# Attention heads with token-major scores and turned probabilities, every second head of two chunks

## The chip, the cores and the metric

The kernel runs on one core of a Trainium2 chip. The metric is the device time of one execution in microseconds (us), the median of three runs.

## The reference

A transformer block whose layer norms are modulated by a condition vector: attention of 2048 tokens over a cached window of keys and values, then a gated feed-forward part.

```python
mod = (_silu(c) @ w_mod).reshape(c.shape[0], 6, 1, -1)      # sa, ca, ga, sb, cb, gb
h = _layernorm(x, axis=-1) * (1 + ca) + sa
q = (h @ wq)                       # 2048 tokens, 32 heads of 128
k, v = k_cache[:, :, Sk - W:, :], v_cache[:, :, Sk - W:, :]  # 4 kv heads, W = 512 keys
scores = jnp.einsum('bhqd,bhkd->bhqk', q, k) * Dh ** (-0.5)
o = jnp.einsum('bhqk,bhkd->bhqd', _softmax(scores, axis=-1), v)
x = x + ga * (o @ wo)
h = _layernorm(x, axis=-1) * (1 + cb) + sb
x = x + gb * (silu(h @ w_gate) * (h @ w_up) @ w_down)
```

Everything is bfloat16; x is 2048x1024, wq 1024x4096, wo 4096x1024, the feed-forward width is 3584. Eight query heads share one kv head.

## The kernel before

The 2048 tokens are four chunks of 512. Attention comes first, chunk by chunk and head by head, in one loop `for i in range(1, NA + 2)` over NA = 128 pairs (chunk i // 32, head i % 32), which is software-pipelined. Iteration i projects q of pair i + 3 (`qproj`), computes the scores of pair i - 1 (`scores`) and the products with v of pair i - 2 (`pv`). After a chunk's last head, `oproj` multiplies by wo and adds to the residual. The feed-forward part follows for all chunks.

- `qproj`: eight matmuls of 128x512 into bank 4 (QB), then VectorE casts them to `qT_s` (L644). q lies feature-major: 128 features x 512 tokens.
- `scores`: four matmuls of 128x512 with a block of 128 keys as the stationary operand, so that the scores are key-major, in banks 0 to 3 (SCB); ScalarE takes the exponential in two instructions of 128x1024 (L813) into `ex_s`.
- `pv`: sixteen matmuls of 128x129. A 128x128 block of the exponentials is stationary, and v with a column of ones moves, so that the output is token-major and its last column is the sum of the exponentials. VectorE takes the reciprocal (L831) and multiplies (L834) out of banks 5 and 6; a DMA transpose (L837) brings the 512x128 result into `oT_all`, feature-major.
- `load_wq` fetches the weights for four heads (1 MB), `load_mt` and `mod_col` compute the late modulation columns beside attention (a DMA transpose from w_mod, then a VectorE reduction), and `run_bg` advances the layer norm of the next chunk by one step (`ln_task`, with a DMA transpose of 128x1024, L454).

The order of the work is the order in which the Python program records it; each engine, and the SP queue for its DMAs, runs its own instructions strictly in that order. A tracker sets the waits. Each buffer (`_Buf`) keeps the last write recorded and the reads since; in `T.op` a reader waits for that last write:

```python
for b in reads:
    lw = b.last_write
    if lw is not None:
        s, c = lw
        if req.get(s, 0) < c:
            req[s] = c
```

A write waits for the last write and for the reads recorded since it. `absorb` carries such waits over to another buffer that takes the same place in the arena.

Of the kernel before, what the change touches and what calls it, by code (L numbers as in the profile page):

```python
# [7 lines left out]
P = 128  # L8
# [122 lines left out]
def bass_adaLN_cond__sliding_block_cached__swiglu_ffn__prompt_kernel(  # L131
# [63 lines left out]
    rstd = [rstd4[:, i:i + 1] for i in range(4)]  # L195
    bq = S_("bq", [P, 8], F32)
    rl = [S_("rl%d" % i, [P, 4], F32) for i in range(2)]
    nsc = [S_("nsc%d" % i, [P, D], BF16) for i in range(2)]
    tmp = [S_("tmp%d" % i, [P, 512], F32) for i in range(2)]

    KB = 1024
    A_BYTES = 162 * KB
# [19 lines left out]
    def bank(b, n=512, off=0):  # L222
        return ps[:, b * 512 + off:b * 512 + off + n]
# [19 lines left out]
    B_mv = [_Buf("mv%d" % i) for i in range(4)]  # L243
    B_rs = [_Buf("rs%d" % i) for i in range(4)]
    B_rl = [_Buf("rl%d" % i) for i in range(2)]
    B_ns = [_Buf("ns%d" % i) for i in range(2)]
    B_tmp = [_Buf("tmp%d" % i) for i in range(2)]
    B_h2 = [[_Buf("h2_%d_%d" % (s, dt)) for dt in range(DT)] for s in range(2)]
# [12 lines left out]
    with nc.Block() as block:  # L261

        @block.gpsimd
        def _(g):
# [5 lines left out]
            def mm(out_ap, lhsT, rhs, start, stop, reads, bank_buf, skip=False):  # L270
                T.op(PE, lambda: TE.matmul(out_ap, lhsT, rhs, start=start, stop=stop, skip_group_check=skip),  # L271
                     reads=reads, writes=[bank_buf])
# [368 lines left out]
            def qproj(i, b=QB, k0=0):  # L641
                qproj_mm(i, b, k0, DT)
                qs = q_slot(i)
                T.op(DVE, lambda: V.tensor_copy(qT_s[qs], bank(b)), writes=[PB[b], B_qT[qs]])  # L644
# [160 lines left out]
            def scores(i):  # L805
                ch, h = divmod(i, Hq)
                gk = h // rep
                qs = q_slot(i)
                es = i % NEX
                for kt in range(KT):  # L810
                    mm(bank(SCB + kt), kT_sb[:, gk * KT + kt, :], qT_s[qs], True, True, [B_kT[gk], B_qT[qs]], PB[SCB + kt])
                for kp in range(KT // 2):
                    T.op(ACT, lambda: A.activation(ex_s[es][:, 2 * kp:2 * kp + 2, :], banks2(SCB + 2 * kp), AF.Exp, scale=att_scale),  # L813
                         writes=[PB[SCB + 2 * kp], PB[SCB + 2 * kp + 1], B_ex[es]])

            def pv(i):
                ch, h = divmod(i, Hq)
                gk = h // rep
                es = i % NEX
                os_ = i % NOS  # L820

                for jj in range(2):
                    for kt in range(KT):
                        for jb in range(2):
                            j = 2 * jb + jj
                            b = PVB + jb
                            mm(bank(b, P + 1, jj * 130), ex_s[es][:, kt, j * P:(j + 1) * P], v_aug[:, gk * KT + kt, 0:P + 1],
                               kt == 0, kt == KT - 1, [B_ex[es], B_va, B_vg[gk]], PB[b])
                both = [PB[PVB], PB[PVB + 1]]
                r = i % 2  # L830
                T.op(DVE, lambda: V.reciprocal(rl[r][:, :].rearrange("p (a b) -> p a b", a=2), psap(PVB * 512 + P, [[512, 2], [130, 2]])),  # L831
                     writes=both + [B_rl[r]])
                rlb = bass.AP(tensor=rl[r][:, :].tensor, offset=0, ap=[[4, P], [2, 2], [1, 2], [0, P]])
                T.op(DVE, lambda: V.tensor_tensor(o_s[os_].rearrange("p (a b) d -> p a b d", a=2),  # L834
                                                  psap(PVB * 512, [[512, 2], [130, 2], [1, P]]), rlb, ALU.mult),
                     reads=[B_rl[r]], writes=both + [B_os[os_]])
                T.op(Q_tr[os_], lambda: SP.dma_start_transpose(oT_all[:, h, :].rearrange("p (j q) -> p j q", j=TPC),  # L837
                                                               o_s[os_].rearrange("p j d -> p (j d)")),
                     reads=[B_os[os_]], writes=[B_oT[h]])

            B_wo = [_Buf("wo%d" % i) for i in range(8)]
            wo_s = [None] * 8
# [21 lines left out]
            def oproj_end(ch, k, b):  # L864
                j, hf = divmod(k, 2)
                t = ch * TPC + j
                resid(b, t, hf * 512, 512, 0, k, x_res[:, t, :], B_x[t])
                run_bg(1)

            def oproj(ch):  # L870
                for k in range(2 * TPC):
                    b = [QB, XB][k % 2]
                    oproj_mm(ch, k, b, 0, Hq)
                    oproj_end(ch, k, b)

            ln1 = {}
            ln2 = {}
# [15 lines left out]
            GATER = {19 + n: NGP + n for n in range(DT - NGP)}  # L893
            GATET = {23: 0, 24: 1}
            GATES = {26: 0, 27: 1}
            t2 = Hq + 6 + (9 * (NL - 1)) // 4
            TURNT = (28, t2 + 1)
            PUTT = {33: (0, c_sil, B_csil), 30: (1, mrow[0:DT, :], B_mrow), t2 + 3: (2, mrow[0:DT, :], B_mrow)}
            GETT = {35: (0, sc_row, B_scr), 31: (1, rowb[0][:, :], B_row[0]), t2 + 4: (2, rowb[1][:, :], B_row[1])}
            LOADT = {Hq + 2 + (9 * n) // 4: n for n in range(NL)}  # L900
            LOADO = {5 + (21 * p) // 8: p for p in range(8)}
            LOADK = {1: 1, 5: 2, 6: 3}
            for i in range(1, NA + 2):
                ch, h = divmod(i, Hq)
                if i in LOADK:
                    load_k(LOADK[i])
                if i == 4:
                    load_wq((i + 4) // 4 + 1)
                if 2 <= i < NQ0:
                    q_shifted(i)  # L910
                if i in (2, 3):
                    load_wga(i - 2)
                if i in LOADX:
                    load_x(LOADX[i])
                if i in LOADO:
                    load_wo(LOADO[i])
                if i in GATET:
                    gate_turn(GATET[i])
                if i in TURNT:
                    if i > Hq:  # L920
                        T.op(DVE, lambda: V.tensor_copy(mstg[:, 0:DT], mcol[:, 2 * DT:3 * DT]), reads=[B_mcol], writes=[B_mstg])
                    row_turn()
                if i in PUTT:
                    row_put(*PUTT[i])
                if i in GETT:
                    row_get(*GETT[i])
                if i == 7:
                    add_ln1(1)
                if h == 2 and 1 <= ch < NCH - 1:
                    add_ln1(ch + 1)  # L930
                if h == 2 and ch == NCH - 1:
                    add_ln2(0)
                if i + LEAD < NA:
                    if (i + LEAD) % Hq == 0:
                        finish(ln1[(i + LEAD) // Hq])
                    if i == 1:
                        scores(0)
                    if i in (1, 3, 5):
                        q_bias_mm(i + 1, i + 3, XB)
                    if i > NQ0:  # L940
                        qproj(i + LEAD)
                    elif i % 2 == 1:
                        qproj_mm(NQ0 + i // 2, QB, 0, HK)
                    else:
                        qproj(NQ0 - 1 + i // 2, QB, HK)
                if i - 4 in LOADT:
                    n = LOADT[i - 4]
                    mod_col(n)
                    g0, last = divmod(n, DT)
                    if last == DT - 1:  # L950
                        mod_take(g0, B_late[g0 + 1])
                        if g0 == 1:
                            mod_gain(1, B_late[2], B_g[1])
                n = i - (NA - LEAD)
                if 0 <= n <= 2:
                    oproj_mm(NCH - 1, 0, QB, 8 * n, 8 * n + 8)
                elif n >= 3:
                    oproj_mm(NCH - 1, 1, XB, 8 * (n - 3), 8 * (n - 3) + 8)
                if 1 <= i - 1 < NA:
                    scores(i - 1)  # L960
                if 0 <= i - 2 < NA:
                    pv(i - 2)
                    ch2, h2 = divmod(i - 2, Hq)
                    if i % 4 == 1 and i > 5:
                        load_wq((i + 4) // 4 + 1)
                    if i in LOADT:
                        load_mt(LOADT[i])
                    if h2 == Hq - 1 and ch2 < NCH - 1:
                        oproj(ch2)
                run_bg(1)  # L970
                for n in GATEP.get(i, ()):
                    gate_part(n)
                if i in GATER:
                    gate_row(GATER[i])
                if i in GATES:
                    gate_sum(GATES[i])
                if i == max(GATER):
                    gate_split()
# [152 lines left out]
```

## Time and profile before

| | |
|---|---|
| median of three runs | 1270.05 us (1269.99 to 1270.45) |
| profiled execution | 1270.14 us, of which span 1268.3 us |
| TensorE matmuls (PE) | 1255.1 us busy, 99% of the span |
| VectorE (DVE) | 485.1 us, 38% |
| ScalarE (ACT) | 341.6 us, 27% |
| 128x512 matmuls | 5085 records, mean 380 ns |
| 128x129 matmuls | 2048 records, mean 220 ns |
| DMA transposes of 128x512 (L837) | 128, median 2.6 us from issue to landing |

The span runs from the first to the last instruction of one profiled execution; the 1.8 us around it belong to the execution but to no instruction. Matmuls are pipelined: the duration of one in the table includes its way through the array, and the next one starts before it ends. PE is the matmuls, PEld the weight loads, SPq what the SP queue issues.

### The profile page before, as it was taken

How to read it: one execution, taken by the hardware profiler on the slowest of the kernel's cores; microseconds unless marked ns; L12 is line 12 of the kernel's file. 1: busy time of each engine (PE TensorE's matmuls, PEld its weight loads, DVE VectorE, ACT ScalarE, POOL GpSimd, SP SyncE). 2: the span in 40 equal slices, each digit the busy share in tenths (PEclk: the TensorE clock that was granted, in tenths of full speed). 3: DMA queues.
4: the chain of work that ended last, by engine and by line, in shares of the span. 5: the costliest groups of instructions: out<-in, count | busy, mean ns of one | idle time of the engine just before them, and what ended most of it. 6: DMA issues, size and time to landing. Idle time of an engine off the chain costs nothing.

```text
span 1268.3 us, 17609 instructions
## 1 busy us (share of the span) xinstructions
PE 1255.1 (99%) x7442; PEld 640.7 (51%) x7583; DVE 485.1 (38%) x894; ACT 341.6 (27%) x389; POOL 56.0 (4%) x95
## 2 busy tenths in 40 slices
PE   8999999999999999999999999999999999999999
PEld 5655545555455554555544444444444444444444
DVE  4676226764257641365322321233212321222122
ACT  4655205553035550155510111011100111011100
POOL 1530000000000000000000000000000000000000
PEclk9999999999999999999999999999999999999999
DMA  9998306875029641064243972055512644034200
GB/s 320 264 263 218 92 1 127 177 171 125 1 57 177 138 114 34 9 129 123 61 145 100 291 246 94 25 158 150 168 40 72 177 141 134 17 128 154 67 9 25
DMA packets 239997, 156.67 MB, mean 124 GB/s; under 512 B 133296, under 2 KB 225840, under 8 KB 239920
## 3 DMA queue, kind: packets, MB, share of 16 engines
q1 hardware_dynamic: 181664, 96.83, 31.6%
q10 hardware_dynamic: 58256, 58.73, 14.6%
q8 instruction: 59, 0.97, 0.3%
q14 instruction: 18, 0.15, 0.1%
HBM read 119.93 MB, written 4.20 MB: 98 GB/s over the span
## 4 chain that ended last, share of the span: by engine, by line
PE 98%; issue 1%; DMA 0%; SPq 0%; DVE 0%
PE ps L271 98%; DMA arena<-in_w_mod_dram 0%; SPq L309 0%; SPq L334 0%; PE ps L275 0%; DVE arena L496 0%; DVE tmp L853 0%; DVE arena L855 0%; DVE gain_f L486 0%
## 5 line engine op out<-in xcount | busy, mean ns | idle before, releaser
L271 PE MATMUL ps<-arena 128*128 128x512 bf16 (+1 forms) x7213 | 1249.3, 333 | 10.1 <-POOL arena L298 2.0
L271 PEld LDWEIGHTS ps<-arena 128*128 128x128 bf16 x7354 | 632.9, 98 | 621.5 <-issue 2.1
L813 ACT ACTIVATE arena<-ps 128x1024 bf16<-128x1024 f32 x256 | 261.9, 1023 | 345.1 <-PE ps L271 333.4
L1059 ACT ACTIVATE arena<-ps 128x512 bf16<-128x512 f32 x112 | 66.9, 597 | 499.6 <-PE ps L271 499.6
L1060 DVE TENSOR_TENSOR arena<-ps,arena 128x512 bf16<-128x512 f32 x112 | 77.5, 692 | 276.2 <-PE ps L271 276.2
L853 DVE TENSOR_TENSOR tmp<-ps,rowb 128x512 f32<-128x512 f32 (+1 forms) x65 | 44.4, 683 | 318.8 <-PE ps L271 318.8
L644 DVE CAST arena<-ps 128x512 bf16<-128x512 f32 x120 | 82.8, 690 | 47.7 <-PE ps L271 47.7
L834 DVE TENSOR_TENSOR arena<-ps,rl 128x512 bf16<-128x512 f32 x128 | 88.5, 691 | 4.7 <-DVE rl L831 0.2
L831 DVE RECIPROCAL rl<-ps 128x4 f32<-128x4 f32 x128 | 23.4, 182 | 114.1 <-PE ps L271 114.1
L429 POOL TENSOR_SCALAR rstd<-mv 128x1 f32<-128x1 f32 x28 | 6.1, 216 | 910.3 <-DVE mv L428 910.3
L424 DVE BATCH_NORM_STATS2 st<-x_res 128x6 f32<-128x512 bf16 x62 | 42.4, 683 | 3.4 <-DMA x_res<-in_A_x_dram 3.3
L593 DVE SCALAR_TENSOR_TENSOR arena<-arena 128x1024 bf16<-128x1024 bf16 x24 | 29.2, 1215 | 0.0
L855 DVE TENSOR_TENSOR arena<-tmp,x_res 128x512 bf16<-128x512 f32 (+2 forms) x33 | 22.3, 677 | 1.1
L855 DVE TENSOR_TENSOR x_res<-tmp,x_res 128x512 bf16<-128x512 f32 x32 | 22.2, 693 | 1.1
L440 DVE TENSOR_SCALAR arena<-arena,gain,mod_bf 128x512 bf16<-128x512 bf16 x56 | 21.2, 420 | 0.0
L435 DVE TENSOR_SCALAR nsc<-x_res,mv,rstd 128x1024 bf16<-128x1024 bf16 x30 | 19.2, 641 | 0.0
L431 POOL TENSOR_TENSOR rstd<-rstd,mhalf 128x1 f32<-128x1 f32 x28 | 15.7, 559 | 2.3
L772 POOL TENSOR_SCALAR arena<-arena,sc_bf 128x512 f32<-128x512 bf16 x8 | 12.9, 1614 | 0.5 <-POOL arena L774 0.2
L774 POOL TENSOR_TENSOR arena<-arena 128x512 f32<-128x512 f32 x8 | 10.1, 1265 | 0.7
L428 DVE BATCH_NORM_AGGREGATE mv<-st 128x2 f32<-128x12 f32 x28 | 5.8, 209 | 1.0
L271 PEld LDWEIGHTS ps<-sc_bf,arena 128*128 128x128 bf16 x128 | 4.4, 96 | 1.4 <-DMA arena<-in_w_mod_dram 0.3
L271 PE MATMUL ps<-sc_bf,arena 128*128 128x1 bf16 x128 | 4.7, 164 | 0.3 <-DMA arena<-in_w_mod_dram 0.3
(56 smaller groups left out, 59.4 us busy)
## 6 DMA issues: line engine op xcount, KB each, us to landing
arena<-in_A_wq_dram SPq DMA_DIRECT2D x30, 1024.0 KB, 5.8
arena<-in_B_w_gate_dram ACTq DMA_DIRECT2D x28, 1024.0 KB, 5.4
arena<-in_B_w_up_dram ACTq DMA_DIRECT2D x28, 1024.0 KB, 7.9
arena<-in_A_wo_dram SPq DMA_DIRECT2D x8, 1024.0 KB, 7.6
arena<-in_B_w_down_dram SPq DMA_DIRECT2D x7, 1024.0 KB, 8.3
out_dram<-arena SPq DMA_DIRECT2D x15, 256.0 KB, 2.0
x_res<-in_A_x_dram SPq DMA_DIRECT2D x3, 1024.0 KB, 7.0
arena<-arena SPq DMA_TRANSPOSE x132, 2.6
```

The lines of the kernel that those rows point to most:

```text
L271: T.op(PE, lambda: TE.matmul(out_ap, lhsT, rhs, start=start, stop=stop, skip_group_check=skip), reads=reads, writes=[bank_buf])
L424: T.op(DVE, lambda: V.bn_stats(st_[sl][:, hf * 6:hf * 6 + 6], x_res[:, t, hf * 512:hf * 512 + 512]), reads=[B_x[t]], writes=[B_st[sl]])
L440: T.op(DVE, lambda: V.tensor_scalar(dst[:, dt, :], dst[:, dt, :], gain[gi][:, dt:dt + 1], mod_bf[:, ccol + dt:ccol + dt + 1], op0=ALU.mult ...
L593: T.op(DVE, lambda: V.scalar_tensor_tensor(mt[n % 2], mt[n % 2], 1.0, sc_row, op0=ALU.mult, op1=ALU.mult, accum_out=mcol[:, n:n + 1]), rea ...
L644: T.op(DVE, lambda: V.tensor_copy(qT_s[qs], bank(b)), writes=[PB[b], B_qT[qs]])
L813: T.op(ACT, lambda: A.activation(ex_s[es][:, 2 * kp:2 * kp + 2, :], banks2(SCB + 2 * kp), AF.Exp, scale=att_scale), writes=[PB[SCB + 2 * k ...
L831: T.op(DVE, lambda: V.reciprocal(rl[r][:, :].rearrange("p (a b) -> p a b", a=2), psap(PVB * 512 + P, [[512, 2], [130, 2]])), writes=both + ...
L834: T.op(DVE, lambda: V.tensor_tensor(o_s[os_].rearrange("p (a b) d -> p a b d", a=2), psap(PVB * 512, [[512, 2], [130, 2], [1, P]]), rlb, A ...
L853: T.op(DVE, lambda: V.tensor_tensor(tmp[s][:, 0:n], bank(b, n), rowb[ri][:, c0:c0 + n], ALU.mult), reads=[B_row[ri]], writes=[PB[b], B_tmp ...
L855: T.op(DVE, lambda: V.tensor_tensor(dst[:, c0:c0 + n], tmp[s][:, 0:n], x_res[:, t, c0:c0 + n], ALU.add), reads=[B_tmp[s], B_x[t]], writes= ...
L1059: T.op(ACT, lambda: A.activation(sg_s[ss], bank(gb), AF.Silu), writes=[PB[gb], B_sg[ss]])
L1060: T.op(DVE, lambda: V.tensor_tensor(guT[:, ft, :], bank(ub), sg_s[ss], ALU.mult), reads=[B_sg[ss]], writes=[PB[ub], B_gu[ft]])
```

## The change

For every second head of the last two chunks (pairs 66, 68, ..., 126, the set `NAT`) the scores are computed token-major: a 128-token block of q is stationary, and the 512 keys move. ScalarE takes the exponential in four instructions of 128x512 and sums each row on the way (`accum_out`). VectorE takes the reciprocals of the sums and multiplies the probabilities with them, in two halves (`nat_norm`), and one DMA transpose of 128x2048 turns all of them (`nat_turn`). The products (`nat_pv`) then are four matmuls of 128x512 with a 128x128 block of v as the stationary operand; their output is feature-major, so ScalarE copies it straight into `oT_all`, and the transpose of the output goes away for these heads. Iteration i turns pair i and records the products of pair i - 4.

Two places hold probabilities before the turn (`pn`: the arena's `ex_s[0]` and the residual's `tmp`), two slots hold turned ones (`pt`); `p_slot` alternates between them. `pt_region` moves the two slots to another part of the arena at pairs 66, 86 and 96. At a chunk's seam (i = 65, 97) the scores of the next such pair lie inside `oproj`. `load_mt` starts one iteration earlier and then comes every second iteration, and from i = 65 on `load_wq` is recorded ahead of the scores.

```diff
+            NAT0 = 2 * Hq + 2
+            NAT = set(range(NAT0, NA, 2))
+            B_pn = [[_Buf("pn0_%d" % hf) for hf in range(2)], B_tmp]
+            pn = [None, tmp_t[:, :].bitcast(BF16)]
+            Q_pt = [dq("q_pt%d" % i) for i in range(2)]
+            def p_slot(i):
+                return (i - NAT0) // 2 % 2
+            def pt_region(off):
+                pt_over[:] = B_oT[24:] if off == OFF_OT + 24 * KB else []
+                for s in range(2):
+                    B_pt[s] = _Buf("pt%d" % s)
+                    pt[s] = arena.at(off + s * 4 * KB, [TPC * KT, P], BF16, [B_pt[s]])
+            def nat_scores(i):
...
+                for j in range(TPC):
+                    mm(bank(SCB + j), qT_s[qs][:, j * P:(j + 1) * P],
+                       kT_sb[:, gk * KT:(gk + 1) * KT, :].rearrange("p a b -> p (a b)"), True, True,
+                       [B_kT[gk], B_qT[qs]], PB[SCB + j])
+                for j in range(TPC):
+                    T.op(ACT, lambda: A.activation(pn[s][:, j * 512:(j + 1) * 512], bank(SCB + j), AF.Exp, scale=att_scale,
+                                                   accum_out=psum[s][:, j:j + 1]),
+                         writes=[PB[SCB + j], B_pn[s][j // 2], B_psum[s][j // 2]])
+            def nat_norm(i, hf):
+                s = p_slot(i)
+                T.op(DVE, lambda: V.reciprocal(pinv[s][:, 2 * hf:2 * hf + 2], psum[s][:, 2 * hf:2 * hf + 2]),
+                     reads=[B_psum[s][hf]], writes=[B_pinv[s][hf]])
+                for j in (2 * hf, 2 * hf + 1):
+                    pj = pn[s][:, j * 512:(j + 1) * 512]
+                    T.op(DVE, lambda: V.tensor_scalar(pj, pj, pinv[s][:, j:j + 1], None, op0=ALU.mult),
+                         reads=[B_pinv[s][hf]], writes=[B_pn[s][hf]])
+            def nat_turn(i):
+                s = p_slot(i)
+                pt_of[i] = (pt[s], B_pt[s], list(pt_over))
+                T.op(Q_pt[s], lambda: SP.dma_start_transpose(pt[s], pn[s]), reads=B_pn[s], writes=[B_pt[s]])
+            def nat_pv(i):
...
+                pa, pb, over = pt_of.pop(i)
+                ptv = pa.rearrange("p (j k) q -> p j k q", j=TPC)
+                for kt in range(KT):
+                    mm(bank(PVB).rearrange("p (j q) -> p j q", j=TPC), v_aug[:, gk * KT + kt, 0:P], ptv[:, :, kt, :],
+                       kt == 0, kt == KT - 1, [B_va, B_vg[gk], pb], PB[PVB])
+                T.op(ACT, lambda: A.activation(oT_all[:, h, :], bank(PVB), AF.Copy), writes=[PB[PVB], B_oT[h]])
...
-            LOADT = {Hq + 2 + (9 * n) // 4: n for n in range(NL)}
+            LOADT = {Hq + 1 + 2 * n: n for n in range(NL)}
+            PTAT = {2 * Hq + 2: OFF_OT + 24 * KB, 2 * Hq + 22: OFF_H20, 3 * Hq: OFF_HT}
...
+                if i % 4 == 1 and i >= NAT0 - 1:
+                    load_wq((i + 4) // 4 + 1)
...
+                seam = (i - 1) % Hq == 0 and i + 1 in NAT
+                if i + 1 in PTAT and not seam:
+                    pt_region(PTAT[i + 1])
+                if i in NAT and (i - 2) % Hq:
+                    nat_norm(i, 1)
+                    nat_turn(i)
+                nat = i % 2 == 1 and i + 1 in NAT
+                if nat and not seam:
+                    if i - 4 not in LOADT:
+                        run_bg(1)
+                    nat_scores(i + 1)
-                if 1 <= i - 1 < NA:
+                if 1 <= i - 1 < NA and i - 1 not in NAT:
                     scores(i - 1)
                 if 0 <= i - 2 < NA:
-                    pv(i - 2)
+                    if i - 4 in pt_of:
+                        nat_pv(i - 4)
+                    if i - 2 not in NAT:
+                        pv(i - 2)
+                    if (i - 2) % Hq == Hq - 1 or i == NA:
+                        for n in sorted(pt_of):
+                            if n < i:
+                                nat_pv(n)
+                    if nat and not seam:
+                        nat_norm(i + 1, 0)
...
-                        oproj(ch2)
+                        oproj(ch2, [lambda: nat_scores(i + 1), lambda: (nat_norm(i + 1, 0), nat_norm(i + 1, 1))] if seam else ())
+                        if seam:
+                            if i + 1 in PTAT:
+                                pt_region(PTAT[i + 1])
+                            nat_turn(i + 1)
```

## The prediction

> **What bounds the kernel now.** I read the page's engine table and its chain of waits first, then TensorE's waits, the groups by shape, the timeline of one attention iteration, and the landing times of the transposes.
>
> ```profile
> PE 1255.1 (99%) x7442; PEld 640.7 (51%) x7583; DVE 485.1 (38%) x894; ACT 341.6 (27%) x389; POOL 56.0 (4%) x95
> ...
> PE 98%; issue 1%; DMA 0%; SPq 0%; DVE 0%
> ```
>
> ```profile
> PE ps L271 <- POOL arena L298: 2.0, 1, 2.0
> PE ps L271 <- DVE arena L496: 0.6, 1, 0.6
> PE ps L271 <- DMA arena<-in_w_mod_dram: 0.3, 1, 0.3
> ```
>
> TensorE is the bound everywhere: 99% busy, 98% of the chain, and 2.9 us of waits in the whole span, all at the start. A change gains only by taking away TensorE time. It loses whatever it makes TensorE wait, because nothing else is on the path.
>
> ```profile
> 601.07 0.18 DVE L831 RECIPROCAL rl<-ps 128x4 f32<-128x4 f32 x1 [1.08 <-PE ps L271]
> 601.28 0.69 DVE L834 TENSOR_TENSOR arena<-ps,rl 128x512 bf16<-128x512 f32 x1
> 602.00 1.19 SPq L837 DMA_TRANSPOSE arena<-arena  x1
> 602.80 0.69 DVE L644 CAST arena<-ps 128x512 bf16<-128x512 f32 x1 [0.82 <-PE ps L271]
> 603.23 2.14 ACT L813 ACTIVATE arena<-ps 128x1024 bf16<-128x1024 f32 x2 [1.36 <-PE ps L271]
> 604.57 0.18 DVE L831 RECIPROCAL rl<-ps 128x4 f32<-128x4 f32 x1 [1.08 <-PE ps L271]
> ```
>
> This is one iteration of attention in the timeline: start, duration, engine, instruction. From RECIPROCAL to RECIPROCAL it lasts 3.50 us. The chain has 49 matmuls of 128x512 in 10.74 us (from 138.11); the last takes its own 0.38, so one step is (10.74 - 0.38)/48 = 0.216 us. Twelve of them (eight for the next q, four scores) are 2.59 us. The remaining 0.91 us are sixteen 128x129 products at 57 ns. RECIPROCAL starts about 0.20 us after the last product's step, so the iteration begins at E = 600.87. The CAST of q then runs from E+1.93 to E+2.62.
>
> **What is saved.** 31 heads (66, 68, ... 126) replace sixteen products (0.91 us) by four of 128x512 (0.86 us). That is 0.044 us a head, 31 x 0.044 = 1.4 us in all. The scores keep four matmuls of 512 columns. The gain is bounded there: a tenth of a per cent, less than the 0.2% (2.5 us) that a measurement of this kernel tells from no change.
>
> **What is added to TensorE's path: a wait.** This is the step that sets the forecast. There are two slots of turned probabilities, and `p_slot` gives heads i-4 and i the same one. In an even iteration the loop records `nat_turn(i)` first and `nat_pv(i-4)` after it. The tracker makes a reader wait for the last write recorded for its buffer, and that is now the turn of head i, not of head i-4. So the products meant to run four iterations behind wait for a transpose issued in their own iteration. I counted iterations by the slots: 70 to 84 (8), 90 to 94 (3) and 102 to 126 (13), 24 in all. At 86, 88 and 96 the slots have just moved to another place (`pt_region`), so the older turn is the last one written there; 66, 68, 98 and 100 have no product to make.
>
> What the turn waits for, in an even iteration beginning at E (the odd one began at E-3.50):
> - In the odd iteration VectorE ends the regular head's RECIPROCAL and TENSOR_TENSOR 4.61 us after its start, at E+1.11 (3.70 + 0.18 + 0.03 + 0.69). Then come `nat_norm(i,0)`'s reciprocal (0.18) and two 128x512 multiplies. The nearest row is this one, and I take its 0.41 us:
>
> ```profile
> L435 DVE TENSOR_SCALAR arena<-x_res,mv,rstd 128x512 bf16<-128x512 bf16 x2 | 0.8, 410 | 0.8 <-POOL rstd L528 0.8
> L541 ACT ACTIVATION_READ_ACCUMULATOR arena<-x_res,nmean 128x1 f32 x1 | 0.2, 186 | 0.0
> L1059 ACT ACTIVATE arena<-ps 128x512 bf16<-128x512 f32 x112 | 66.9, 597 | 499.6 <-PE ps L271 499.6
> ```
>
> - With 0.03 us between dependent instructions (1.06 us in all) that ends at E+2.20, so the q CAST, queued behind it, is done at E+2.92. Then `nat_norm(i,1)`, another 1.06 us: E+4.0. In the eight iterations of chunk 2 before i = 86 a `mod_col` (1.22 + 0.08) stands in the queue too and adds 0.25.
> - ScalarE is not late: its four exps of 0.60 + 0.19 us (the rows above) end 5.3 us after the odd iteration's start, E+1.8.
> - SP issues at E+4.03. SP is free by then: the regular head's transpose takes 1.19 and `load_mt` 1.3 from E+1.1 on, together to E+3.6.
> - The landing of a 128x2048 transpose is in no row. Nearest:
>
> ```profile
> L837 SPq DMA_TRANSPOSE arena<-arena x128: 1188/1192/2657, 35.0 to 639.6; - x128
> ...
> DMA to landing us min/median/max: 2.4/2.6/8.1
> ```
>
> ```profile
> L454 SPq DMA_TRANSPOSE arena<-nsc x28: 1232/1250/2732, 57.0 to 1018.1; - x28
> ...
> DMA to landing us min/median/max: 3.1/5.1/7.5
> ```
>
> These are 128x512 and 128x1024. Undisturbed, 2.4 and 3.1 us: twice the data costs 0.65 more, so four times gives about 4.35 at least. Two 128x1024 transposes issued back to back at 206.01 and 207.36 are down by 210.7, 4.7 us for the same data. Four of 128x512 in a row, 3 x 1.19 + 2.4 = 6.0, is the upper end. I take 4.5, between the first two, since it is one issue.
>
> Landing is at E+8.53; TensorE is ready at E+2.59. With 0.03 to wake and the mean of the 0.25 (0.08), the wait is 6.05 us. 24 x 6.05 = 145 us. Queued behind the waiting product on TensorE is everything: the next q, the next scores, the regular products. Nothing covers it.
>
> **Smaller additions.** At i = 97 three heads are finished in a row through one bank: `nat_pv(94)` waits for the regular head's eviction (0.20 + 0.18 + 0.03 + 0.69 = 1.1), the next for ScalarE's copy of the last (0.38 + 0.04 + 0.60 less the step, 0.8) and for turn 96, due about then: 1.9 us. At i = 128 the copy again, 0.8. Together 2.7. VectorE's and ScalarE's extra work (31 times a net 1.2 and 1.7 us), and the 31 dropped o transposes, lie inside iterations that the wait makes longer. `load_mt` every second iteration and the moved `load_wq` stay off the path: VectorE needs some 3.0 us of each 3.50 in chunk 1.
>
> **TensorE's pace after a wait.** Between 3.2 and 5.6 us, after the idle start, matmuls are slow; 0.38 us is their normal duration:
>
> ```profile
> L271 PE MATMUL ps<-arena 128*128 128x512 bf16 x6 | 2.7, 630 | 0.0
> ```
>
> Twelve of them fill 4.34 us from 3.10, where 11 x 0.216 + 0.38 = 2.75 would do; counted from the first at 2.02 the loss is about 2.1 us. A later gap of 0.55 us (at 10.65) is followed by normal durations. A 6 us gap lies between these rows: 0 to 2.1 us a stall. I take half, 1.05, as neither row is nearer: 25 us in 24 stalls.
>
> By the Trainium skill (TensorE: Matmul & The Clock Gate, "What's actually happening") the array halves its clock after an idle window of about 3.4 us and frees it after a busy one. By that a 6 us gap holds a whole window about three times in four, and the sum would be an estimated 13 us higher. No row in the span shows such a fall, only the slow start.
>
> **The sum.** The profiled execution took 1270.1 us (span 1268.3 and 1.8 around it), the median 1270.05. 1270.1 - 1.4 + 145 + 2.7 + 25 = 1442 us.
>
> **Rivals.**
> - *No loss of pace.* The gaps are too short to slow the array: 1270.1 - 1.4 + 145 + 2.7 = 1416 us. For it: nothing in the span shows a fall. Against: the start does run slow.
> - *Full loss of pace.* Each stall pays what the start paid, 24 x 2.1 = 50: 1467 us. The skill's rule above stands nearest to this one.
> - *A slow transpose.* Landing in 6.0 us or more; the maxima of 8.1 and 7.5 show what a neighbour's traffic can do. The stall is 7.55, 24 x 7.55 = 181: 1477 us with half the pace loss, 1502 with all. Against: the added `load_wq` traffic (5.8 us to landing) starts with the odd iteration and is down before the turn starts.
> - *No wait: not slower.* The products wait for the turn of four iterations before, as the change's words have it. Then 14 us cover a chain that ends 8.5 us after E, and 1270.1 - 1.4 + 2.7 = 1271.4 us remains, within 0.2%. It decides from the turn of head i: if TensorE doesn't need it until E+17, all 145 us and the pace loss vanish. Against it is the order of recording alone, but that I read as certain.
>
> **How the numbers follow.** Forecast 0.52, no pace loss 0.15, full pace loss 0.17, slow transpose 0.12, no wait 0.04. Low end: landing 4.35 and multiplies of 0.35 (row L675: 348 ns) make the stall 5.65, 136 us, with no pace loss: 1407. High end: the slow transpose with all the pace loss, 1502. I give 1405 to 1502. Slower by over 0.2% holds all but the no-wait case: 0.96; same 0.03; faster 0.01, since 1.4 us alone doesn't reach 0.2%.
>
> **What would show it.** Right: TensorE's waits list some 24 for a DMA (arena<-arena or arena<-tmp), about 6 us each, in chunks 2 and 3; heads 82, 84 and 92 have none; TensorE's busy share near 88%; granted clock below 1.00 from 530 us on. Each L896 issue lands in 4.4 to 4.7 us. Wrong: no such waits, or a share of these waits naming VectorE or ScalarE.

## The result, and the profile after

The changed kernel takes 1450.13 us (median of five runs, 1448.90 to 1451.89) beside 1270.05 us: a ratio of 1.1415 [1.1399, 1.1431]. The forecast of 1442 was 8 us short. The profiled execution took 1451.89 us, with a span of 1450.1 us and a mean granted clock of 0.962.

The page's engine table, chain of waits and clock row of the changed kernel (the clock in tenths, one digit for each fortieth of the span):

```profile
PE 1308.9 (90%) x7211; PEld 633.0 (44%) x7211; DVE 506.3 (35%) x1018; ACT 378.5 (26%) x606; POOL 56.0 (4%) x95
...
PEclk9999999999888889998988999999999999999999
...
PE 83%; DMA 9%; DVE 7%; issue 0%; ACT 0%; SPq 0%; ACTq 0%
```

TensorE is busy for 53.8 us longer and yet only 90% of the time; DMA now holds 9% of the chain and VectorE 7%. The clock row falls below 9 in eight slices between the 11th (from 362.5 us) and the 22nd (to 797.6 us), which is where the token-major heads are. TensorE's waits say on what (total us, times, longest):

```profile
PE ps L276 <- DMA arena<-arena: 70.6, 13, 7.9
PE ps L276 <- DMA arena<-tmp: 58.1, 11, 5.8
PE ps L276 <- ACT arena L907: 2.9, 3, 1.4
PE ps L276 <- POOL arena L303: 2.0, 1, 2.0
PE ps L280 <- DVE nsc L440: 1.6, 2, 1.3
PE ps L276 <- DVE arena L841: 1.0, 1, 1.0
PE ps L276 <- DMA arena<-in_A_wq_dram: 1.0, 2, 0.7
PE ps L276 <- DVE pinv L886: 0.9, 1, 0.9
```

13 + 11 = 24 waits for a transpose out of the two places `pn`, together 128.7 us, 5.36 each. The view of the turn's own line (L896) has both sides of it, the landing and who waited:

```profile
L896 SPq DMA_TRANSPOSE arena<-arena x16: 1532/1960/4108, 363.5 to 802.6; - x16
L896 SPq DMA_TRANSPOSE arena<-tmp x15: 1719/1932/2909, 375.0 to 789.6; - x15
...
PE ps L276: 128.7, 24
...
DMA to landing us min/median/max: 4.3/4.3/6.2
```

One stall in the timeline, in chunk 3 (start, duration, engine, instruction, idle time before it and what ended that):

```profile
677.20 0.69 DVE L841 TENSOR_TENSOR arena<-ps,rl 128x512 bf16<-128x512 f32 x1
...
677.99 0.74 DVE L890 TENSOR_SCALAR tmp<-tmp,pinv 128x512 bf16<-128x512 bf16 x2
...
678.71 0.69 DVE L649 CAST arena<-ps 128x512 bf16<-128x512 f32 x1
...
679.50 0.74 DVE L890 TENSOR_SCALAR tmp<-tmp,pinv 128x512 bf16<-128x512 bf16 x2
...
680.27 1.72 SPq L896 DMA_TRANSPOSE arena<-tmp  x1
...
684.62 3.40 PE L276 MATMUL ps<-arena 128*128 128x512 bf16 x8 [5.09 <-DMA arena<-tmp]
```

It is the chain of the forecast in its order: the regular head's eviction, the first half of the norm, the cast of q, the second half, SP's issue 0.03 us later, and 4.35 us on TensorE begins. The eight matmuls behind the wait take 3.40 us: a step of some 0.43 us, where 0.216 is the normal one. So the kernel loses twice at each of these places, by the wait and by the pace after it. The experiments separate the two.

### The profile page after: what moved, and what is told of

Its sections match the earlier page's. It is cut to its first block, busy times and chain, and to the rows that moved or that the text cites. A ratio compares the mean times of both kernels' runs of the same rounds, so it can differ in the third digit from the quotient of the medians.

```text
span 1450.1 us, 17431 instructions
## 1 busy us (share of the span) xinstructions
PE 1308.9 (90%) x7211; PEld 633.0 (44%) x7211; DVE 506.3 (35%) x1018; ACT 378.5 (26%) x606; POOL 56.0 (4%) x95
## 4 chain that ended last, share of the span: by engine, by line
PE 83%; DMA 9%; DVE 7%; issue 0%; ACT 0%; SPq 0%; ACTq 0%
PE ps L276 83%; DMA arena<-arena 4%; DMA arena<-tmp 3%; DVE arena L649 1%; DVE arena L841 1%; DVE arena L890 1%; DMA arena<-in_A_wq_dram 1%; DVE tmp L890 1%; DVE arena L598 0%; DVE st L429 0%; DVE rl L838 0%; DVE pinv L886 0%; DMA x_res<-in_A_x_dram 0%; SPq L593 0%; ACT arena L820 0%
## 5 line engine op out<-in xcount | busy, mean ns | idle before, releaser
L276 PE MATMUL ps<-arena 128*128 128x512 bf16 (+2 forms) x6982 | 1303.7, 350 | 137.1 <-DMA arena<-arena 70.6
L276 PEld LDWEIGHTS ps<-arena 128*128 128x128 bf16 x6982 | 625.4, 99 | 809.7 <-DMA arena<-arena 77.0
L820 ACT ACTIVATE arena<-ps 128x1024 bf16<-128x1024 f32 x194 | 198.7, 1024 | 275.7 <-PE ps L276 266.6
L1159 ACT ACTIVATE arena<-ps 128x512 bf16<-128x512 f32 x112 | 66.9, 597 | 500.2 <-PE ps L276 500.2
L841 DVE TENSOR_TENSOR arena<-ps,rl 128x512 bf16<-128x512 f32 x97 | 67.1, 692 | 3.4
L907 ACT ACTIVATE arena<-ps 128x512 bf16<-128x512 f32 x31 | 18.5, 596 | 138.0 <-PE ps L276 138.0
L838 DVE RECIPROCAL rl<-ps 128x4 f32<-128x4 f32 x97 | 17.7, 183 | 92.2 <-PE ps L276 92.2
L880 ACT ACTIVATE arena<-ps 128x512 bf16<-128x512 f32 x64 | 37.9, 595 | 44.1 <-PE ps L276 41.2
L880 ACT ACTIVATE tmp<-ps 128x512 bf16<-128x512 f32 x60 | 35.6, 595 | 31.6 <-PE ps L276 28.8
L890 DVE TENSOR_SCALAR arena<-arena,pinv 128x512 bf16<-128x512 bf16 x64 | 22.6, 353 | 2.3
L890 DVE TENSOR_SCALAR tmp<-tmp,pinv 128x512 bf16<-128x512 bf16 x60 | 21.2, 353 | 2.1
```

The lines of the kernel that those rows point to most:

```text
L880: T.op(ACT, lambda: A.activation(pn[s][:, j * 512:(j + 1) * 512], bank(SCB + j), AF.Exp, scale=att_scale, accum_out=psum[s][:, j:j + 1]), ...
L890: T.op(DVE, lambda: V.tensor_scalar(pj, pj, pinv[s][:, j:j + 1], None, op0=ALU.mult), reads=[B_pinv[s][hf]], writes=[B_pn[s][hf]])
L1159: T.op(ACT, lambda: A.activation(sg_s[ss], bank(gb), AF.Silu), writes=[PB[gb], B_sg[ss]])
```

## The experiments

**e1_order: the turn recorded behind the products.** Nothing is left out; the last norm half and the turn move behind `nat_pv(i-4)`, so that the products' last recorded write is the turn of their own head.

```diff
-                if i in NAT and (i - 2) % Hq:
-                    nat_norm(i, 1)
-                    nat_turn(i)
...
                     if i - 4 in pt_of:
                         nat_pv(i - 4)
+                    if i in NAT and (i - 2) % Hq:
+                        nat_norm(i, 1)
+                        nat_turn(i)
```

> The changed kernel with nat_norm(i,1) and nat_turn(i) recorded behind nat_pv(i-4), so that the products wait for the turn of four iterations before; nothing else. Theory (the loss is the wait for the turn of the same iteration, and the slow pace after it): the 24 waits for a DMA vanish, the granted clock is 1.00, and the time is 1270.1 - 1.4 + 2.7 = 1271.4 us, within 1270 to 1274. Rival (the new form itself costs: more VectorE, ScalarE and SP work, and four times the transposed data): most of the 180 us stays, over 1350 us.

Measured: 1279.17 us (four executions, 1276.22 to 1280.46), 1.0065 [1.0051, 1.0078] of the kernel before. TensorE's waits in the profiled execution, the slowest of the four:

```profile
PE ps L276 <- ACT arena L907: 3.0, 3, 1.5
PE ps L276 <- POOL arena L303: 2.0, 1, 2.0
PE ps L276 <- DMA arena<-in_A_wq_dram: 2.0, 1, 2.0
PE ps L276 <- DVE arena L841: 1.1, 1, 1.1
PE ps L276 <- DVE pinv L886: 0.9, 1, 0.9
PE ps L276 <- DVE arena L501: 0.6, 1, 0.6
PE ps L276 <- DMA arena<-in_w_mod_dram: 0.2, 1, 0.2
```

All 24 waits for a turn are gone, and 171 us with them: the order of recording is the cause. What is left is 8.7 us more than before and 7.8 more than I had expected. In the profiled execution, which is 10.0 us above the kernel before, 3.0 + 1.1 us are seams, where finished heads go through one bank; 2.0 us are a wait for the weights of q, 0.9 for the first norm; some 3 us are pace. The windows of the seam at i = 97 (length, busy time of PE, PEld, DVE, ACT and POOL with instructions, granted clock, DMA share, GB/s):

```profile
474.00:478.20 4.20, 2.33 (x23) 1.35 (x22) 1.57 (x3) 0.60 (x1) 0.00 (x0) 1.00 1.02 204
478.30:485.00 6.70, 6.01 (x15) 1.95 (x14) 0.00 (x0) 0.60 (x1) 0.00 (x0) 0.50 0.36 103
```

Behind gaps of 1.09 and 0.78 us the clock is at a half for 6.8 us; a third gap, of 0.69 us, lies inside that stretch. The other three executions have a granted clock of 1.000, which has no room for such a stretch (it makes 0.997 here), and yet they take 1276.22, 1278.80 and 1279.54 us. So pace is no part of the median's 8.7 us: the waits less the 1.4 us saved make 5.6 of it, and some 3 us stay open.

**e2_fill22, e3_fill8: the gap filled with work that nobody reads.** The wait stays as it is, but N matmuls of 128x512 into a free bank stand ahead of each waiting product: TensorE is kept busy while the turn is under way. Results are as in the changed kernel.

```diff
                     if i - 4 in pt_of:
+                        if i < NA and pt_of[i - 4][1] is B_pt[p_slot(i)]:
+                            for _ in range(22):      # 8 in e3_fill8
+                                mm(bank(PVB + 1), kT_sb[:, 0, :], kT_sb[:, 0:KT, :]..., True, True, [B_kT[0]], PB[PVB + 1])
                         nat_pv(i - 4)
```

> The changed kernel with 22 matmuls of 128x512, whose result nobody reads, ahead of the products in each of the 24 iterations that wait (22 x 0.216 = 4.75 us of a wait of about 5.1). Theory (of the 181 us, 129 are waits and some 54 are matmuls at half pace after them): the array stays busy, the clock stays at 1.00, the landing of the turn sets the time as before, and 54 us go: 1396 us. Rival (the clock has no part; what is lost is wait alone, and the busy time is an artefact of records): 1450 us, or more.

Measured: 1411.54 us, 1.1116 [1.1099, 1.1133], granted clock 0.999. Its waits for turns:

```profile
PE ps L276 <- DMA arena<-arena: 9.9, 12, 3.2
PE ps L276 <- DMA arena<-tmp: 5.9, 11, 0.8
```

22 useless matmuls in each of 24 places make the kernel 38.6 us faster. That is what the lost pace costs, 1.6 us a stall. The clock records agree: in the changed kernel's profile there are 24 slow stretches, one at each wait, TensorE is busy for 86.9 us in them, and at half clock half of that is lost, 43 us; e2_fill22 has one left, which costs 1.7 us. My 54 us was the growth of the page's busy time, and that was a wrong measure: the trace of the kernel before has 7442 matmuls for 7583 weight loads, so records are missing and its busy time is too short. Beside e4_seam (below), which has the same matmuls as the changed kernel, all 7211 recorded, at full clock, the busy time grows by 46 us (1262.9 to 1308.9). The wait alone is then e2_fill22 less e1_order, 132 us, or 5.5 us a stall; TensorE's waits in the profile, which begin at the end of the last matmul and not at its step, make 128.7.

> The same with 8 matmuls, 1.73 us of the wait; an idle gap of 3.3 to 3.8 us remains. Theory A (the clock falls only after a whole idle window of 3.4 us, as the changes of clock 3.41, 6.83 and 10.24 us apart suggest): most gaps no longer hold a window, the clock is above 0.99, and the time is 1396 to 1405 us, about as with 22. Theory B (the loss goes with the length of the gap): a third of the loss goes, 1450 - 54 x 1.73/5.3 = 1432 us.

Measured: 1448.36 us, 1.1405 [1.1388, 1.1421], clock 0.967. Eight matmuls take 1.7 us out of each gap and win nothing that can be told. The same window, two iterations long, in the changed kernel and then in e3_fill8:

```profile
686.00:699.65 13.65, 8.60 (x46) 3.91 (x45) 4.24 (x11) 5.29 (x11) 0.00 (x0) 0.88 0.49 110
```

```profile
686.00:699.65 13.65, 10.34 (x54) 4.70 (x52) 3.79 (x11) 5.30 (x13) 0.00 (x0) 0.87 0.36 67
```

There are eight more matmuls in the 13.65 us, and the clock is down as much. In the clock records of both kernels every slow stretch lasts 3.41, 6.83 or 10.24 us, whole multiples of one window of 3.413 us; both have 24 of them, and a pair of iterations in chunk 3 settles at 13.65 us, four such windows, with one slow stretch in each pair.

**e5_fill14, e6_fill18: between the two.** The same edit with 14 and 18.

> The changed kernel with 14 unread matmuls ahead of each waiting product (3.02 us), so that 2.1 to 2.6 us of the wait stay idle, after 22 matmuls took away all slow pace (1411.5 us) and 8 none of it (1448.4). Theory A (a window of 3.4 us that is idle for about two thirds slows the clock too, as the cold stretch behind three short gaps at the seam of e1_order suggests): many of the gaps still slow the array, granted clock about 0.97 to 0.98, 1425 to 1448 us. Theory B (only a wholly idle window does): no gap can hold one, granted clock above 0.99, 1411 to 1415 us.

> The same with 18 matmuls (3.88 us), 1.2 to 1.7 us of the wait idle, 35 to 50% of a window. Theory A (about two thirds idle is what it takes): hardly any fall, 1411 to 1418 us. Rival (a third is enough): still over 1425 us.

Measured: 1440.24 us, 1.1323 [1.1306, 1.1340] with 14, and 1411.93 us, 1.1114 [1.1099, 1.1128] with 18. The span and mean granted clock of 8, 14 and 18 fillers:

```profile
core 0: 1444.9 us, clock 0.967
```

```profile
core 0: 1438.6 us, clock 0.975
```

```profile
core 0: 1410.3 us, clock 0.996
```

With 14, gaps of 2.0 to 2.6 us are left at most places, and the clock falls at 19 of the 24; with 18, gaps of 1.1 to 1.8 us are left at most, and none of these costs anything (there are three slow stretches, two behind gaps of 3.95 and 2.83 us and one behind the gaps of the seam).

What decides is the idle time inside one window. In each trace all the slow stretches begin on one grid of 3.413 us. Laid over TensorE's gaps between 320 and 830 us, in the seven traces that have slow stretches there (the changed kernel, e1_order, the four fills and e10_half_fill16 below), every window outside a slow stretch that holds 2.02 us or more of idle time is followed by half pace, and none that holds less than 1.78 us is. In between both occur: 1.78 us at the seam of e6_fill18 was followed, 1.93 us in e1_order was not. A gap of 2.32 us in e5_fill14 cost nothing, since it lay in two windows with 1.66 and 0.66 us. So the step lies between 1.8 and 2.0 us of idle time in one window, a little over half of it.

It is a step: four more matmuls a stall are worth 28 us, the eight of e3_fill8 were worth nothing that can be told. With 0, 8, 14, 18 and 22 useless matmuls there are 24, 24, 19, 3 and 1 slow stretches, and half of TensorE's busy time in them is 43, 40, 34, 5 and 2 us; less that, all five kernels take 1406 to 1410 us.

**e10_half_fill16: half the data.** 16 fillers, and the turn moves only the first half of the probabilities (128x1024); the other half of the slot isn't written, so its time is that of a smaller transfer.

```diff
-                T.op(Q_pt[s], lambda: SP.dma_start_transpose(pt[s], pn[s]), ...)
+                T.op(Q_pt[s], lambda: SP.dma_start_transpose(pt[s][:, 0:TPC * KT // 2, :], pn[s][:, 0:TPC * KT // 2 * P]), ...)
```

> The changed kernel with 16 unread matmuls ahead of each waiting product, as in the runs with 18 and 22, and each turn moves only the first half of the probabilities (128x1024): the second half of what the products read is left out. Theory (the landing of the turn stands whole in each of the 24 waits, and nothing else ends them): landing 3.1 instead of 4.3 us, 24 x 1.2 = 29 us less than the full turn with a steady clock: 1411.7 - 29 = 1383 us. Rival (the wait ends by VectorE's or SP's backlog, not by the landing): 1405 us or more.

Measured: 1379.04 us, 1.0851 [1.0834, 1.0867], clock 0.999. The turn in it:

```profile
L896 SPq DMA_TRANSPOSE arena<-arena x16: 1231/1233/1953, 362.6 to 733.4; - x16
...
DMA to landing us min/median/max: 3.0/3.1/4.1
```

It takes 32.9 us less than e6_fill18. Some 3 us of that are pace (one slow stretch here, three there: 1.7 and 4.7 us by the clock records), so the wait is 30 us shorter, 1.25 a stall, for a landing that is 1.2 us shorter. The landing stands whole in the wait, as the sum had it.

**e4_seam: the seams mended as well.** e1_order, and the head that is finished at a chunk's seam gets the other bank in the next iteration.

```diff
-            def nat_pv(i):
+            def nat_pv(i, b=PVB):
...
-                    if (i - 2) % Hq == Hq - 1 or i == NA:
-                        for n in sorted(pt_of):
-                            if n < i:
-                                nat_pv(n)
+                    if i % Hq == 0 and i - 2 in pt_of:
+                        nat_pv(i - 2, PVB + 1)
```

> e1_order, and at the end of a chunk the two last products no longer stand in a row in one bank: nat_pv(94) and nat_pv(126) are recorded one iteration earlier in bank 6, and nat_pv(96), which belongs to the next chunk, stays with its turn at i = 100. Theory (the seams cost 2.7 us of e1_order, the four wide products save 1.4 us): 1268.7 us, 0.1% below the kernel before and 2 to 3 us below e1_order. Rival (there is no gain in four matmuls of 512 columns over sixteen of 129): 1270 us or above.

Measured: 1272.12 us, 1.0013 [1.0005, 1.0022], clock 1.000. The seams were worth 7.1 us, where I had put 2.7 in the forecast and 2 to 3 here: 4.1 us are the four gaps of e1_order's profile (1.09, 0.78, 0.69 and 1.51), and the rest stays open, as three of e1_order's four executions lost no pace. The waits for q's weights stay (1.4 us in two), and the timeline shows why: SP is behind in chunk 2.

```profile
409.11 0.57 SPq L362 DMA_DIRECT2D arena<-in_A_wq_dram  x1
...
411.08 2.54 SPq L593 DMA_TRANSPOSE arena<-in_w_mod_dram  x1
...
413.74 3.14 SPq L896 DMA_TRANSPOSE arena<-arena  x1
...
419.64 2.89 SPq L896 DMA_TRANSPOSE arena<-tmp  x1
...
423.93 0.57 SPq L362 DMA_DIRECT2D arena<-in_A_wq_dram  x1
```

A turn holds SP for 2.9 and 3.1 us here, `load_mt` for 2.5, and the weight loads start 14.8 us apart, where four iterations last 14.0.

**e7_wq_act, e8_norms: SP relieved.** e7_wq_act is e4_seam with the later weight loads issued on ScalarE's queue; e8_norms is e7_wq_act with both norm halves in the even iteration, behind the cast.

```diff
+                late = gidx > 2 * HG + 2
-                T.op(Q_wq[sl], lambda: SP.dma_start(
+                T.op(Q_wqa[sl] if late else Q_wq[sl], lambda: (A if late else SP).dma_start(
```

> e4_seam with the weights of the last two chunks (load_wq from the 19th on) issued from ScalarE's queue instead of SP's. Theory (in chunk 2 the SP queue has fallen behind: its turns take 2 to 3 us each to issue, four iterations of issues take 15.2 us where TensorE takes 14, and the weights land late by 1.4 us in all): those waits go, 1272.1 - 1.4 = 1270.7 us. Rival (the weights land late because the turns' packets fill the DMA engines, whoever issues): 1272 us still.

> e7_wq_act, and both halves of nat_norm recorded in the even iteration, behind the q cast, so that no half stands ahead of the next cast on VectorE. Theory (the 0.94 us gap at the first such head is the cast queued behind a half that waits for its exponentials, and 1.4 us of narrower products are real): 1270.1 - 1.4 = 1268.7 to 1269.3 us, below the kernel before by 0.1%. Rival (the turn now comes a microsecond later and the next exponentials or the SP queue wait for it): 1271 us or more.

Measured: 1275.70 us, 1.0043 [1.0031, 1.0055], and 1274.26 us, 1.0033 [1.0021, 1.0046]: both slower than e4_seam, and scattered (1270.26 to 1278.93). The waits for weights are gone from e7_wq_act and the 0.9 us for the norm from e8_norms, but exponentials now wait for turns. From e8_norms:

```profile
404.00 5.58 SPq L899 DMA_TRANSPOSE arena<-tmp  x1
...
405.91 0.60 ACT L883 ACTIVATE arena<-ps 128x512 bf16<-128x512 f32 x1 [4.44 <-DMA arena<-arena]
```

This turn's issue lasted 5.58 us (out of `tmp` the median is 4.9 in this kernel and the longest 7.1), and ScalarE stood 4.44 us for a `pn` that the turn before had not yet read. Two of the reasons are only argued: that the two queues' descriptors stand in each other's way, and that this makes the scatter. That moving the loads doesn't pay is shown.

**e9_late, e11_chunk3: fewer heads.** On e4_seam, with the weights on SP and both norm halves behind the cast: the new form only from head 88 on (20 heads), and only in the last chunk, entered at the seam (15 heads).

```diff
-            NAT0 = 2 * Hq + 2
-            NAT = set(range(NAT0, NA, 2))
+            NAT0 = 2 * Hq + 22                   # e11_chunk3: 3 * Hq + 2, NAT as it was
+            NAT = set(range(NAT0 + 2, NA, 2))
```

> e4_seam with the new form only from head 88 on (20 heads, after the last load_mt), and both halves of nat_norm behind the q cast; the weights stay on SP. Theory (in chunk 2 the load_mt transposes and the turns together fill the SP queue and the DMA engines, whichever queue carries the weights; without load_mt there is room): no wait beyond those of the kernel before, and 20 x 0.044 = 0.9 us are kept: 1270.5 - 0.9 = 1269.6 us. Rival (the turns alone crowd the queue, in chunk 3 too): 1271 us or more.

> e9_late with the new form in the last chunk alone (15 heads, 98 to 126), entered at the seam, where the first new scores stand between two output projections. Theory (each new head saves 0.04 us, as a pair of iterations of 6.95 instead of 6.99 us shows; the entry at head 88 cost 1.0 us of waits for ScalarE, the entry at a seam costs none): 1270.4 - 15 x 0.044 = 1269.7 us, a ratio of 0.9995, at the edge of what can be told. Rival (another entry cost appears): 1270.4 us or more.

Measured: 1271.23 us, 1.0006 [0.9998, 1.0015], and 1269.99 us, 0.9995 [0.9986, 1.0004], beside 1270.38 and 1270.46 for the kernel before on the same chip. Inside e9_late a pair of iterations lasts 6.95 us by the casts of q, where it is 6.99 before: 0.04 us a head, as the forecast said. Its entry costs more than that, because eight score matmuls fall into one iteration there:

```profile
PE ps L276 <- ACT tmp L880: 1.0, 3, 0.4
```

With 0.9 us saved and 1.0 waited, another 0.7 us of e9_late's time stays open.

e11_chunk3 has no such entry. Its engine table:

```profile
PE 1255.1 (99%) x7265; PEld 633.4 (50%) x7403; DVE 496.0 (39%) x954; ACT 357.9 (28%) x494; POOL 56.0 (4%) x95
```

15 x 0.044 = 0.7 us were to be had, 0.5 were measured, and the interval holds no change. So no version beats the kernel before by what a measurement of it can tell.

## Why the prediction was right

**What was right.** TensorE was the bound, the gain was bounded at 1.4 us, and the wait came from the order of recording: 24 waits for DMAs, none at the three heads whose slots had moved, 171 us gone when one block of three lines moved down (e1_order). The rival without a wait fell with the first trace, and so did the slow transpose (landing 4.3 us median). The rival without a loss of pace fell with e2_fill22. The signs came near: 5.4 us a wait for "about 6", 90% for 88%, a landing of 4.3 us for 4.4 to 4.7. "Granted clock below 1.00 from 530 us on" was a slip: chunk 2, where the heads begin, starts at 360 us.

**The wait was too large: 145 us, measured 132.** In the timeline, counted from E = 676.78: the first norm half is done at E+1.95 (2.20 in the forecast), the cast at E+2.62 (2.92), SP issues at E+3.49 (4.03), the products start at E+7.84 (8.53). The norm was the term: each half took 0.84 us where the forecast had 1.09. A multiply was taken at 0.41 us from a row with another purpose, and the trace has 0.353, which is 0.12 a half; the rest is the reciprocal, 0.15 us for 0.18, which in the trace starts 0.09 us before the instruction ahead of it ends (679.31 beside 679.40), where the forecast had 0.03 after it.

```profile
L890 DVE TENSOR_SCALAR arena<-arena,pinv 128x512 bf16<-128x512 bf16 x64 | 22.6, 353 | 2.3
```

From SP's issue to the first product it was 4.35 us, 0.15 shorter than the 4.5 taken, and the trace lets TensorE's wait begin 0.16 us later, at the end of its last matmul. The lower bounds given for both rows, 0.35 and 4.35, were the right values.

**The pace was too small: 25 us, measured 38.6.** Half of the start's loss was taken, as neither of two rows lay nearer, so the 1.05 us a stall was a guess. In fact every one of the 24 stalls pays, 1.6 us each, about midway between that and the 2.1 of the rival with full loss, because the gap of 5.1 us is over twice the idle time that suffices. The estimate by the Trainium skill (TensorE: Matmul & The Clock Gate, "What's actually happening"), 13 us above the forecast's, gives 38 us, and the measurement agrees in the sum, by luck. It differs in the mechanism: the Trainium skill has the clock fall after an idle window of about 3.4 us, by which an estimated half of the measured gaps of 5.1 us, (5.1 - 3.41)/3.41, would hold a whole one. The traces have windows of 3.41 us, but 2.0 us idle inside one were enough (e5_fill14), and once two gaps of 1.09 and 0.78 us (e1_order).

**The small additions were too small: 2.7 us.** e1_order shows 8.7 us net of the 1.4 saved, some 10 in all: 4.1 us of gaps at the seams, 2.0 for the weights and 0.9 for the first norm; some 3 stay open. At the seams 0.69 us for a third head and 0.7 more at i = 128 were missed. Beyond them the step that failed is "the moved `load_wq` stay off the path", by way of "SP is free by then": I gave SP 1.2 and 1.3 us for the issues that I had rows for, and nothing for the turn itself, which holds it for 1.5 to 4.1 us. In the changed kernel the long iterations hide that, except at the first stall (i = 70), where a `load_mt` holds SP for 2.51 us, the turn is issued 2.6 us after the last multiply, and TensorE waits 7.90 us; in e1_order it costs 2.0 us of waiting for weights.

**The sum by the runs.** 1270.4 (before, on the experiments' chip) + 8.7 + 132 + 38.6 = 1450. These terms are differences between runs and must add up; the changed kernel's own profile gives 1270.1 - 1.4 + 128.7 (waits for turns) + 43 (pace by the clock records) + 7 (its other waits) = 1448, beside 1451.9 for that execution. The forecast's errors, -13, +14 and +7, largely cancelled: that the total came within 8 us, closer than its terms, was luck.

## What to carry to other kernels

Where a tracker lets a reader wait for the last recorded write of its buffer, a two-slot pipeline needs the reader of the old contents recorded before the writer of the new; check this in the recorded order before costing anything else. A stall of TensorE costs more than its length: find how much idle time the clock tolerates, and fill or shorten gaps to below that, as less than that gains little (here 8 useless matmuls nothing, 14 some 10 us, 18 and 22 over 38). Before a saving of 0.04 us a head is worth building, add up what its entry, its seams and the issue time of its DMAs cost.

## What the runs showed of the hardware

- **Shortening a gap can win nothing.** From 5.1 to some 3.4 us of gap the loop kept its period of 13.65 us, four clock windows; with gaps of 1.1 to 1.8 us nearly all of the lost pace came back at once.
- **A gap need not fill a window to slow the clock.** 2.02 us or more of idle time in one window of 3.41 us always did so, less than 1.78 us never. A gap that straddled two windows could be longer and cost nothing (2.32 us in e5_fill14), and two short ones in one window could add up (1.09 and 0.78 us in one execution of e1_order).
- **A large transpose is slow to issue, not only to land.** One of 128x1024 held SP for 1.23 us at the median (e10_half_fill16), one of 128x2048 for 1.9 to 2.0 and at most 4.1 us in the changed kernel, at most 7.1 in e8_norms with weight loads on a second queue. The landing grew from 3.1 to 4.3 us.
